# One core, Sinkhorn-sorted block attention into a max-of-two expert layer: the kernel rebuilt with the sort's data stationary, no DRAM scratch and the experts as a linear part plus one ReLU

## The chip, the cores and the metric

The kernel runs on one core of a Trainium2 chip. The metric is the device time of one execution in microseconds. A profile is one execution recorded by the hardware profiler. Names used below: TensorE (PE; its loads of the stationary operand are listed as PEld), VectorE (DVE), ScalarE (ACT), GpSimd (POOL), SyncE (SP). TensorE multiplies a stationary operand, loaded first, with a moving one and writes to PSUM; DVE and ACT take the result from there ("evacuate" it). DMAs are issued from the queues of SP, ACT and POOL; POOL's here also convert float32 to bfloat16.

## The reference

```python
# q, k, v: (4, 8, 768, 64); sort_net: (4, 8, 8, 8); eight blocks of 96 rows
P = sort_net
for _ in range(5):
    P = np.exp(P - np.max(P, axis=-1, keepdims=True))
    P = P / (np.sum(P, axis=-1, keepdims=True) + 1e-09)
    P = P / (np.sum(P, axis=-2, keepdims=True) + 1e-09)
k_sorted = np.einsum('bhij,bhjcd->bhicd', P, k_b)      # v_sorted likewise
scores = scale * q_b @ k_sorted^T                       # inside each block of 96
attn = softmax(scores);  out = attn @ v_sorted
x = out.transpose(0, 2, 1, 3).reshape(3072, 512)
h1 = x @ w1;  h2 = x @ w2                               # (512, 1024) each
return np.maximum(h1, h2) @ w_out                       # (1024, 512), float32
```

## The kernel before

There are 32 groups (batch and head) of 8 blocks. **Sinkhorn** (L69 to L85): all 32 groups on partitions, five rounds of one exp on ACT and six small operations on DVE. **Block-diagonal matrices** (L87 to L98): each group's 8x8 matrix is put on the diagonal of one of two 128x128 tiles (16 groups each) by a DMA of its own, 32 in all, from SP and ACT. **Sort** (`emit_sort_batch`, L142): rows of k and v (16 groups x 8 blocks = 128 partitions, a block's 96 x 64 elements along the row) are the moving operand in pieces of 512 columns, the block-diagonal tile the stationary one. The result, `sort_ps`, has blocks on partitions, which attention cannot use; it is evacuated (k by ACT, L176, v by DVE, L179), written to a DRAM scratch in bf16 (L181) and read back with the 96 rows of a block on partitions (`k_grp` L207, `v_grp` L215).

**Attention** (`emit_attention_group`, L197), a group at a time: four transposes of q (`tq_ps`, L224) and four of k (`tk_ps`, L236), copied by DVE; then twice four scores matmuls (`sc_ps`, L252), one exp on ACT (L260), four matmuls with v and a column of ones (`o_ps`, L264), whose last column is the row's sum, and copy, reciprocal and multiply on DVE (L272 to L274) into `x_stage`. After a batch's eight heads, `emit_x_transpose` (L283) makes `xT`, with the model dimension on partitions.

**Experts**: `emit_moe_h` (L300) takes 512 tokens and 128 of the 1024 hidden columns: four matmuls of 512 columns with w1 (L305), four with w2 (L313), a copy of h1 on ACT (L321), the maximum on DVE (L323). `emit_moe_out` (L326) multiplies with w_out in eight matmuls (L331), copies on ACT (L339) and stores 128 rows. The expert work of finished batches is dealt between the attention of the next ones, one unit at each half group; what is left runs after the last batch. The order on each engine is set by the framework's scheduler from this program order; PSUM has three pools (three sort or h tiles, three transposes or scores, two outputs).

## Time and profile before

| | |
|---|---|
| time, median of three runs | 294.71 us (292.66 to 296.38) |
| span of the profiled execution, first to last instruction | 290.0 us |
| PE busy | 211.6 us, 73%, 1520 matmuls |
| DVE, ACT, POOL busy | 116.6, 99.3, 40.4 us |
| HBM read, written | 31.47 MB, 12.58 MB |

The profiled execution's own time is its span of 290.0 us; the median of the runs is 4.7 us above it. The profile's page cuts the span into 40 slices of 7.25 us and gives the busy share of each engine in tenths, and the clock that TensorE was granted ("PEclk", 9 is full, 5 is half). Rows of a group read: line, engine, operation, what it writes and reads, shapes, count, then busy us, mean ns of one, and the idle time of the engine before them with who ended it. Matmuls are pipelined, so a single one's length contains latency; the pace is read from many in a row.

### The profile page before, as it was taken

What the parts mean: (1) busy time and instruction counts of PE and PEld (TensorE: products, weight loads), DVE (VectorE), ACT (ScalarE), POOL (GpSimd) and SP (SyncE); (2) the same over time, 40 slices, a digit from 0 to 9 for tenths busy, and PEclk for the clock granted to TensorE, in tenths of its full rate; (3) what the DMA queues carried; (4) which work ended last, traced back from release to release, by engine and by line L of the source; (5) the groups of instructions that cost most, each with busy time, mean ns of one, the idle gap of its engine ahead of it and who ended that gap; (6) DMA issues with size and microseconds to landing.
All of it is one profiled execution on the core that took longest, in us unless ns stands there. A gap on an engine that the chain in (4) does not pass through costs nothing.

```text
span 290.0 us, 4264 instructions
## 1 busy us (share of the span) xinstructions
PE 211.6 (73%) x1520; PEld 107.2 (37%) x1520; DVE 116.6 (40%) x393; ACT 99.3 (34%) x198; POOL 40.4 (14%) x66
## 2 busy tenths in 40 slices
PE   0001424235238589998879999999999999999994
PEld 0000000012024365554446455455455554444441
DVE  5400004323027872675352756365645640430320
ACT  2000421003312235434346343357444374333322
POOL 8300402106320121112111212112000000000000
PEclk9999955557555755999997999999999999999999
DMA  9993699999999997546883465754421003003003
GB/s 66 176 213 63 124 218 260 218 180 187 220 219 232 187 139 61 58 57 68 128 141 43 54 70 54 147 109 48 51 75 72 2 0 132 14 0 146 0 27 120
DMA packets 90245, 31.75 MB, mean 109 GB/s; under 512 B 77424, under 2 KB 84592, under 8 KB 90224
## 3 DMA queue, kind: packets, MB, share of 16 engines
q0 software_dynamic: 29120, 12.59, 36.2%
q1 hardware_dynamic: 30576, 9.45, 14.7%
q10 hardware_dynamic: 30528, 9.44, 14.4%
q8 instruction: 12, 0.20, 0.3%
q14 instruction: 9, 0.07, 0.1%
HBM read 31.47 MB, written 12.58 MB: 152 GB/s over the span
## 4 chain that ended last, share of the span: by engine, by line
PE 61%; DMA 24%; DVE 6%; ACT 5%; issue 2%; ACTq 1%; SPq 0%; DVEq 0%
PE h_ps L305 15%; PE moe_o_ps L331 15%; PE h_ps L313 14%; DMA k_sorted_dram<-k_ck 8%; PE o_ps L264 5%; DMA bd<-p_bf 5%; PE sc_ps L252 5%; DMA v_grp<-v_sorted_dram 4%; DMA k_grp<-k_sorted_dram 4%; PE xt_ps L287 3%; DMA v_sorted_dram<-v_ck 2%; PE tk_ps L236 2%; ACT e_sb L260 2%; DVE v_ck L179 1%; ACT k_ck L176 1%
## 5 line engine op out<-in xcount | busy, mean ns | idle before, releaser
L305 PE MATMUL h_ps<-xT,w_sb 128*128 128x512 bf16 x192 | 55.2, 390 | 0.0
L323 DVE TENSOR_TENSOR g_sb<-h_ps,h_sb 128x512 bf16<-128x512 f32 x48 | 33.1, 691 | 53.6 <-PE h_ps L313 51.6
L313 PE MATMUL h_ps<-xT,w_sb 128*128 128x512 bf16 x192 | 53.0, 380 | 0.0
L260 ACT ACTIVATE e_sb<-sc_ps 96x384 bf16<-96x384 f32 x64 | 30.1, 486 | 47.0 <-PE sc_ps L252 34.2
L331 PE MATMUL moe_o_ps<-wout,g_sb 128*128 128x512 bf16 x192 | 44.5, 379 | 0.7 <-ACT o_sb L339 0.7
L321 ACT CAST h_sb<-h_ps 128x512 bf16<-128x512 f32 x48 | 28.2, 588 | 47.8 <-PE h_ps L305 47.6
L164 PE MATMUL sort_ps<-k_ld,bd 128*128 128x512 bf16 x24 | 12.1, 562 | 37.3 <-DMA bd<-p_bf 20.3
L264 PE MATMUL o_ps<-v_grp,e_sb 96*96 96x65 bf16 x256 | 24.7, 224 | 11.6 <-DMA v_grp<-v_sorted_dram 6.4
L203 POOL DMA_DIRECT2D q_grp<-in_q_dram x24 | 18.5, 773 | 104.0 <-PE tq_ps L224 60.4
L179 DVE CAST v_ck<-sort_ps 128x512 bf16<-128x512 f32 x24 | 15.6, 685 | 41.7 <-PE sort_ps L164 34.7
L264 PEld LDWEIGHTS <-e_sb 96*96 96x96 bf16 x256 | 19.9, 138 | 30.1 <-ACT e_sb L260 13.9
L176 ACT CAST k_ck<-sort_ps 128x512 bf16<-128x512 f32 x24 | 13.3, 589 | 44.8 <-DMA bd<-p_bf 19.6
L274 DVE TENSOR_TENSOR x_stage<-o_ps,rs_sb 96x256 bf16<-96x256 f32 x64 | 26.7, 418 | 1.1
L331 PEld LDWEIGHTS <-g_sb 128*128 128x128 bf16 x192 | 18.4, 98 | 21.3 <-issue 1.6
L339 ACT COPY o_sb<-moe_o_ps 128x512 f32<-128x512 f32 x24 | 14.1, 586 | 35.2 <-PE moe_o_ps L331 35.1
L164 PEld LDWEIGHTS <-bd 128*128 128x128 bf16 x48 | 5.4, 121 | 51.8 <-issue 51.6
L313 PEld LDWEIGHTS <-w_sb 128*128 128x128 bf16 x192 | 17.5, 98 | 16.7 <-issue 0.2
L272 DVE COPY rs_sb<-o_ps 96x4 f32<-96x4 f32 x64 | 9.7, 153 | 32.3 <-PE o_ps L264 31.9
L305 PEld LDWEIGHTS <-w_sb 128*128 128x128 bf16 x192 | 17.2, 101 | 13.2 <-issue 0.3
L252 PE MATMUL sc_ps<-qT,kT 64*96 64x96 bf16 x256 | 19.0, 228 | 2.0 <-DVE kT L245 2.0
L252 PEld LDWEIGHTS <-kT 64*96 64x96 bf16 x256 | 12.8, 132 | 17.4 <-DVE kT L245 11.1
L233 DVE COPY qT<-tq_ps 128x384 bf16<-128x384 bf16 x32 | 11.1, 348 | 19.4 <-PE tq_ps L224 19.4
(33 smaller groups left out, 144.5 us busy)
## 6 DMA issues: line engine op xcount, KB each, us to landing
q_grp<-in_q_dram POOLq DMA_DIRECT2D x32, 96.0 KB, 3.3
k_ld<-in_k_dram POOLq DMA_DIRECT2D x6, 512.0 KB, 8.6
v_ld<-in_v_dram POOLq DMA_DIRECT2D x6, 512.0 KB, 11.0
k_sorted_dram<-k_ck SPq DMA_DIRECT2D x24, 128.0 KB
v_sorted_dram<-v_ck ACTq DMA_DIRECT2D x24, 128.0 KB
k_grp<-k_sorted_dram SPq DMA_DIRECT2D x32, 96.0 KB
v_grp<-v_sorted_dram ACTq DMA_DIRECT2D x32, 96.0 KB
out_dram<-o_sb SPq DMA_DIRECT2D x12, 256.0 KB
```

The costliest lines, as they stand in the source:

```text
L164: nc.tensor.matmul(ps, bd_tiles[t], ld[:, sub * SORT_CHUNK : (sub + 1) * SORT_CHUNK], start=True, stop=True,)
L179: nc.vector.tensor_copy(out=ck, in_=ps)
L203: nc.gpsimd.dma_start(out=q_grp, in_=q_g[g].rearrange("(j c) d -> c j d", j=NB))
L252: nc.tensor.matmul(sc_ps[:, sub, :], kT[ii * D : (ii + 1) * D, pr, :], qT[ii * D : (ii + 1) * D, pr, :], start=(sub == 0), stop=(sub == 3),)
L260: nc.scalar.activation(out=e_sb, in_=sc_ps, func=AF.Exp, scale=scale)
L264: nc.tensor.matmul(o_ps[:, sub, :], e_sb[:, sub, :], v_grp[:, i, :], start=(sub == 0), stop=(sub == 3),)
L274: nc.vector.tensor_tensor(out=x_stage[:, par:NB:2, h * D : (h + 1) * D], in0=o_ps[:, :, 0:D], in1=rs_sb.to_broadcast([BLK, 4, D]), op=ALU. ...
L305: nc.tensor.matmul(h1_ps, w_sb[dmt][:, fi * 128 : (fi + 1) * 128], xT[:, dmt, tok0 : tok0 + TCH], start=(dmt == 0), stop=(dmt == 3),)
L313: nc.tensor.matmul(h2_ps, w_sb[dmt][:, DFF + fi * 128 : DFF + (fi + 1) * 128], xT[:, dmt, tok0 : tok0 + TCH], start=(dmt == 0), stop=(dmt ...
L321: nc.scalar.copy(out=h1_sb, in_=h1_ps)
L323: nc.vector.tensor_tensor(out=g_sb, in0=h2_ps, in1=h1_sb, op=ALU.max)
L331: nc.tensor.matmul(o_ps, g_tiles[fi][:, tsi * 128 : (tsi + 1) * 128], wout_sb[fi], start=(fi == 0), stop=(fi == NFT - 1),)
```

## The change

The kernel is rebuilt around the same mathematics. The main parts:

- **Sort.** The block-diagonal matrix becomes the moving operand and the data the stationary one, so that the result comes out transposed. k is loaded with the even heads of eight head pairs on partitions 0 to 63 and the odd ones on 64 to 127. `sort_k` takes one row position at a time, 64 rows x 64 columns stationary against 64x64 moving, alternately for the two halves, into opposite quarters of the output: 384 matmuls; their evacuation puts 16 positions at a time into `kT`. `sort_v` takes one element of the head dimension at a time, 128 x 96 stationary with a step of 64 elements, against 128x128: 128 matmuls into `v_sb`, rows of a block on partitions. The DRAM scratch and the transposes of k are gone.
- **Block-diagonal matrices** come from two small matmuls with a selection matrix and masked multiplies on DVE; the 32 DMAs are gone.
- **q** is loaded in one DMA a batch, six rows to a partition, paired by heads with two DVE copies, and transposed 128 x 128 (24 matmuls a batch).
- **Attention** works on a head pair and four blocks at once: eight scores matmuls (`scores`), one exp over 96x768, eight matmuls with v (`values`), one reciprocal and one multiply; eight transposes for a pair (`x_transposes`), copied by ACT.
- **Experts.** max(h1, h2) = h2 + relu(h1 - h2), so the output is x (w2 w_out) + relu(x (w1 - w2)) w_out. w2 is transposed (32 matmuls), the product formed once (32 matmuls of 512 columns), the difference taken by DVE in place of w1. `moe_h` has four matmuls of 384 columns for each 128 hidden columns and one ReLU for two such; `moe_out` twelve matmuls of 512 columns, four of them with the product.
- **PSUM** is one ring of four tiles of two banks for every use. Who evacuates (`evac`, `pick`) is settled when the program is written out, by running sums of estimated work of ACT and DVE; exps and x copies are always ACT's, the attention's multiplies DVE's.
- **Order** is the program's own, on every engine: batches 0 and 1 of attention with the weight products first, then the expert units of all batches, with the sorts and attention of batches 2 and 3 dealt between the units of batches 0 and 1, and the units of 2 and 3 at the end. The rest of the loads (second half of k and v, q of batches 2 and 3) stand on POOL's queue behind the first ones.

On SP's queue, at the start of the program, before (bd: the block-diagonal tiles; k_sorted_dram: the scratch):

```order
L65 DMA p_sb<-in_sort_net_dram 32x64
L95 DMA bd_107<-p_bf 8x1x8 x8
L95 DMA bd_109<-p_bf 8x1x8 x8
L181 DMA k_sorted_dram<-k_ck 128x512 x12
L207 DMA k_grp<-k_sorted_dram 96x8x64 x8
```

and the whole of SP's queue now:

```order
L580 UNCONDITIONAL_BRANCH
L89 DMA p_sb<-in_sort_net_dram 32x64
L472 DMA out_dram<-o 128x2x512 x11
L468 DMA out_dram<-o_2570 128x512
L468 DMA out_dram<-o_2585 128x512
```

SP is left with the input of Sinkhorn and the stores. What replaces the 32 DMAs stands on DVE, after the last Sinkhorn step (sel: the selection matrix, pe: its product in PSUM, bv and bk: the block-diagonal matrices for v and k):

```order
L176 TENSOR_TENSOR p_bf<-p_sb,colsum 32x64
L185 TENSOR_REDUCE maskJ<-ident 128x8
L193 COPY sel_155<-ident 32x64 x2
L206 TENSOR_TENSOR pm_160<-pe,maskJ 128x64
L213 TENSOR_REDUCE pt_162<-pm_160 128x8
L215 TENSOR_TENSOR bv_164<-mask_101,pt_162 128x128
L222 TENSOR_TENSOR bk_166<-bv_164 128x64
```

The same six kinds follow once more for the second half. On TensorE, the sort before (the last of the first twenty-two sort matmuls, then the transposes of k):

```order
L164 LDWEIGHTS bd_107
L164 MATMUL sort_ps<-v_ld,bd_107 128x512
L236 LDWEIGHTS k_grp
L236 MATMUL tk_ps<-ident,k_grp 128x96
L236 LDWEIGHTS k_grp
```

and now, the end of the key sort, which runs into the scores with no transposes between:

```order
L262 LDWEIGHTS k_raw
L262 MATMUL k_ps<-bk_166,k_raw 64x64
L301 LDWEIGHTS kT
L301 MATMUL s_ps<-qT,kT 96x96
L301 LDWEIGHTS kT
```

The stationary operand is the data now, and a load of it stands ahead of every matmul as before. On TensorE among the experts, the place of an x transpose now (e: the exps, x: the normalized output of attention):

```order
L325 LDWEIGHTS e
L325 MATMUL o_ps<-v_sb,e 96x65
L353 LDWEIGHTS x
L353 MATMUL tx_ps<-ident,x 128x96
L353 LDWEIGHTS x
```

Eight matmuls with v are followed at once by the eight transposes that need their evacuated result; before, the 32 transposes of a batch came in its last group and after it, some of them between matmuls of that group.

The diff, cut to its core (lines of before first, then the new kernel in its own order):

```diff
-    for g in range(G):
-        t, gl = divmod(g, GB)
-        eng = nc.sync if g % 2 == 0 else nc.scalar
-        eng.dma_start(
-            out=bd_tiles[t][8 * gl : 8 * gl + 8, 8 * gl : 8 * gl + 8],
-            in_=p2_bf[g : g + 1, :, :],
-        )
...
-    k_sorted_dram = dram_pool.tile([G * NB, BLKD], BF16, tag="ksd", name="k_sorted_dram")
-    v_sorted_dram = dram_pool.tile([G * NB, BLKD], BF16, tag="vsd", name="v_sorted_dram")
...
-            nc.sync.dma_start(
-                out=k_grp,
-                in_=k_sorted_dram[g * 8 : g * 8 + 8, :].rearrange(
-                    "i (c d) -> c i d", d=D
-                ),
-            )
...
+    psum = ctx.enter_context(tc.tile_pool(name="psum", bufs=4, space=bass.MemoryType.PSUM))
+    ctx.enter_context(tc.manual_schedule())
...
+    load = {"A": 0.0, "D": 0.0}
+    def pick(a_ns, d_ns):
+        if load["A"] + a_ns <= load["D"] + d_ns:
+            load["A"] += a_ns
+            return "A"
+        load["D"] += d_ns
+        return "D"
+    def evac(out_ap, in_ap, n, two_x=False):
+        if pick((200 + n) / 1.2, (130 + (n / 2 if two_x else n)) / 0.96) == "A":
+            nc.scalar.copy(out=out_ap, in_=in_ap)
+        else:
+            nc.vector.tensor_copy(out=out_ap, in_=in_ap)
...
+    k_src = k.rearrange("b (a par) (j c) d -> par (b a) j (c d)", par=2, j=NB)
...
+    load_q(0)
+    load_k(0, 3)
+    ident = const.tile([128, 128], BF16, tag="ident", name="ident")
+    make_identity(nc, ident)
...
+    load_v(0)
+    load_q(1)
+    load_w(w2_sb, moe_w2)
+    load_w(wo_sb, moe_w_out)
+    load_w(w1_sb, moe_w1)
...
+        sel = const.tile([G, 2, 8, NB], BF16, tag=f"sel{sb}", name=f"sel{sb}")
+        src = ident[0:G, sb * 16 : sb * 16 + 16].rearrange("p (gp par) -> p par gp", par=2)
+        for par in range(2):
+            nc.vector.tensor_copy(
+                out=sel[:, par], in_=src[:, par, :].to_broadcast([G, 8, NB])
+            )
+        pe = ps_f32("pe")
+        nc.tensor.matmul(
+            pe[:, 0 : NB * NB],
+            sel.rearrange("p a g j -> p (a g j)"),
+            p_bf.rearrange("p i j -> p (i j)"),
+            start=True,
+            stop=True,
+        )
...
+        nc.vector.tensor_tensor(
+            out=bv,
+            in0=mask16.to_broadcast([128, 16, NB]),
+            in1=pt.to_broadcast([128, NB, 16]).transpose([0, 2, 1]),
+            op=ALU.mult,
+        )
+        bk = const.tile([128, 8, NB], BF16, tag=f"bk{sb}", name=f"bk{sb}")
+        nc.vector.tensor_tensor(out=bk, in0=bv[:, 0:8, :], in1=bv[:, 8:16, :], op=ALU.add)
...
+        for n in range(16):
+            for par in range(2):
+                m = (n + 8 * par) % 16
+                r0 = par * 64
+                nc.tensor.matmul(
+                    ps[r0 : r0 + 64, m * 64 : (m + 1) * 64],
+                    kv[r0 : r0 + 64, t * 16 + m, :],
+                    bd_k[sb][r0 : r0 + 64, :],
+                    start=True,
+                    stop=True,
+                )
+        evac(
+            kT[:, :, t * 16 : (t + 1) * 16],
+            ps.rearrange("p (c m) -> p m c", m=64),
+            1024,
+        )
...
+        for n in range(8):
+            nc.tensor.matmul(
+                ps[0:BLK, n * 128 : (n + 1) * 128],
+                vv[:, :, t * 8 + n],
+                bd_v[sb],
+                start=True,
+                stop=True,
+            )
+        evac(
+            v_sb[:, :, t * 8 : (t + 1) * 8],
+            ps[0:BLK].rearrange("p (d m) -> p m d", m=128),
+            1024,
+        )
...
+        for ii in range(4):
+            i = ih * 4 + ii
+            for h2 in range(2):
+                nc.tensor.matmul(
+                    ps[0:BLK, h2 * 512 + ii * BLK : h2 * 512 + (ii + 1) * BLK],
+                    kT[h2 * 64 : h2 * 64 + 64, gp * 8 + i, :],
+                    qT[b][h2 * 64 : h2 * 64 + 64, hp, :, i * PB : (i + 1) * PB],
+                    start=True,
+                    stop=True,
+                )
...
+        nc.vector.reciprocal(out=rs, in_=ov[:, :, :, 64])
...
+        nc.vector.tensor_tensor(
...
+        nc.scalar.copy(
+            out=xT[:, hp, b * S : (b + 1) * S].rearrange("p (i c r) -> p i r c", r=R, c=PB),
+            in_=ps[:, 0:S].rearrange("p (i r c) -> p i r c", r=R, c=PB),
+        )
...
+            for fb in range(NFB):
+                nc.tensor.matmul(
+                    ps[:, m * 512 : (m + 1) * 512],
+                    w2T[:, fb, dmt * 128 : (dmt + 1) * 128],
+                    wo_sb[:, fb, :],
+                    start=(fb == 0),
+                    stop=(fb == NFB - 1),
...
+    def w_difference(t):
+        nc.vector.tensor_tensor(
+            out=w1_sb[:, 2 * t : 2 * t + 2, :],
+            in0=w1_sb[:, 2 * t : 2 * t + 2, :],
+            in1=w2_sb[:, 2 * t : 2 * t + 2, :],
+            op=ALU.subtract,
+        )
...
+            fb = t * 2 + m
+            for hp in range(HP):
+                nc.tensor.matmul(
+                    ps[:, m * 512 : m * 512 + TCH],
+                    w1_sb[:, hp, fb * 128 : (fb + 1) * 128],
+                    xT[:, hp, tok0 : tok0 + TCH],
+                    start=(hp == 0),
+                    stop=(hp == HP - 1),
+                )
+        g = gpool.tile([128, 2, TCH], BF16, tag="g", name="g")
+        src = ps.rearrange("p (t f) -> p t f", t=2)[:, :, 0:TCH]
+        if pick((200 + 2 * TCH) / 1.2, (130 + 2 * TCH) / 0.96) == "A":
+            nc.scalar.activation(out=g, in_=src, func=AF.Relu)
+        else:
+            nc.vector.tensor_scalar(
+                out=g, in0=src, scalar1=0.0, scalar2=None, op0=ALU.max
+            )
+        g_tiles[b, ch, t] = g
...
+        for hp in range(HP):
+            nc.tensor.matmul(
+                dst,
+                xT[:, hp, tok0 : tok0 + 128],
+                wc[:, hp, :],
+                start=(hp == 0),
+                stop=False,
+            )
+        for fb in range(NFB):
+            nc.tensor.matmul(
+                dst,
+                g_tiles[b, ch, fb // 2][:, fb % 2, off : off + 128],
+                wo_sb[:, fb, :],
+                start=False,
+                stop=(fb == NFB - 1),
+            )
...
+        elif slot == 1:
+            o = opool.tile([128, 2, 512], FP32, tag="o", name="o")
+            evac(o.rearrange("p t n -> p (t n)"), ps, 1024)
+            nc.sync.dma_start(
+                out=out[tok0 - 128 : tok0 + 128, :].rearrange("(t p) n -> p t n", p=128),
+                in_=o,
+            )
...
+        steps = []
+        for u in range(8 + 2):
+            if u < 8:
+                steps.append(lambda u=u: scores(b, u))
+            if u >= 2:
+                steps.append(lambda u=u: values(b, u - 2))
+                if u % 2 == 1:
+                    steps.append(lambda u=u: x_transposes(b, (u - 2) // 2))
+        return steps
+    for half in range(2):
+        q_transposes(0, half)
+    for t in range(6):
+        sort_k(0, t)
+    for u in range(4):
+        scores(0, u)
+    for t in range(8):
+        sort_v(0, t)
+    for u in range(4, 8):
+        values(0, u - 4)
+        scores(0, u)
+        if u % 2 == 1:
+            x_transposes(0, (u - 4) // 2)
+    for half in range(2):
+        q_transposes(1, half)
+    for u in range(4, 8):
+        scores(1, u - 4)
+        values(0, u)
+        if u % 2 == 1:
+            x_transposes(0, u // 2)
+    for t in range(2):
+        w2_transposes(t)
+    for u in range(4, 8):
+        scores(1, u)
+        values(1, u - 4)
+        if u % 2 == 1:
+            x_transposes(1, (u - 4) // 2)
+    for t in range(2):
+        w_product(t)
+    for u in range(4, 8):
+        values(1, u)
+        if u % 2 == 1:
+            x_transposes(1, u // 2)
+    load_q(2)
+    load_k(1, 3)
+    load_v(1)
+    load_q(3)
+    for t in range(2):
+        w_difference(t)
...
+    rest = []
+    for half in range(2):
+        rest.append(lambda half=half: q_transposes(2, half))
+    for t in range(6):
+        rest.append(lambda t=t: sort_k(1, t))
+    for t in range(8):
+        rest.append(lambda t=t: sort_v(1, t))
+    rest += attention_steps(2)
+    for half in range(2):
+        rest.append(lambda half=half: q_transposes(3, half))
+    rest += attention_steps(3)
...
+    units = []
+    for b in range(B):
+        units += [lambda b=b, t=t: moe_h(b, 0, t) for t in range(4)]
+        units += [lambda b=b, t=t: moe_h(b, 1, t) for t in range(4)]
+        units += [lambda b=b, ti=ti: moe_out(b, ti, b == B - 1 and ti >= 4) for ti in range(6)]
+    hold, span = 5, 2 * 14 - 1
+    done = 0
+    for n, unit in enumerate(units):
+        unit()
+        want = len(rest) * max(0, n + 1 - hold) // (span - hold)
+        while done < min(want, len(rest)):
+            rest[done]()
+            done += 1
```

More of the change, by code (lines that the diff above doesn't have):

```diff
@@ L69 @@
+    load_v(0)
[3 more added lines that the diff above has]
+    load_w(w1_sb, moe_w1)
+    rowsum = const.tile([G, NB], FP32, tag="rowsum", name="rowsum")
+    colsum = const.tile([G, NB], FP32, tag="colsum", name="colsum")
+    p_bf = const.tile([G, NB, NB], BF16, tag="p_bf", name="p_bf")
     for it in range(5):
@@ L78 @@
         nc.vector.tensor_tensor(
-            out=p_sb,
+            out=p_bf if it == 4 else p_sb,
             in0=p_sb,
@@ new lines, with scores @@
+    e_tiles, x_tiles = {}, {}
+    def scores(b, u):
+        hp, ih = divmod(u, 2)
+        gp = (b % 2) * 4 + hp
+        ps = ps_f32("s_ps")
+        for ii in range(4):
[5 more added lines that the diff above has]
+                    qT[b][h2 * 64 : h2 * 64 + 64, hp, :, i * PB : (i + 1) * PB],
+                    start=True,
+                    stop=True,
+                )
+        e = epool.tile([BLK, 2, 4 * BLK], BF16, tag="e", name="e")
+        nc.scalar.activation(
+            out=e,
+            in_=ps[0:BLK].rearrange("p (t f) -> p t f", t=2)[:, :, 0 : 4 * BLK],
+            func=AF.Exp,
+            scale=scale,
+        )
+        load["A"] += 800
+        e_tiles[b, u] = e
```

472 lines of the change are left out of this document (192 added, 280 removed).

## The prediction

> **What bounds the kernel now.** I read the page first, then the busy times by stretch, then the chain of waits, then the timeline of TensorE.
>
> ```profile
> span 290.0 us, 4264 instructions
> PE 211.6 (73%) x1520; PEld 107.2 (37%) x1520; DVE 116.6 (40%) x393; ACT 99.3 (34%) x198; POOL 40.4 (14%) x66
> PE   0001424235238589998879999999999999999994
> PEclk9999955557555755999997999999999999999999
> ```
>
> The rows of slices split the span: TensorE (PE) is mostly idle up to about slice 15 and full after it, and in the idle part its granted clock falls to half. Busy times by stretch (columns: stretch, then busy us and instructions of PE, PEld, DVE, ACT, POOL, then granted clock, DMA share, GB/s):
>
> ```profile
> 0.00:113.00 113.00, 43.36 (x275) 21.66 (x276) 36.63 (x135) 25.43 (x53) 26.56 (x48) 0.69 1.07 176
> 99.00:113.00 14.00, 12.07 (x131) 9.77 (x131) 8.68 (x45) 6.04 (x15) 2.31 (x3) 0.50 1.44 116
> 113.00:286.00 173.00, 168.23 (x1248) 85.50 (x1246) 79.94 (x258) 73.28 (x145) 13.88 (x18) 0.98 0.40 66
> ```
>
> For 113 us PE works 43; from 113, where the first expert matmul stands, to 286 it works 168 of 173 at a clock of 0.98. So there are two stages: a first bound by waits, a second bound by PE. The chain of waits names the first one's (start, length, what):
>
> ```profile
> 11.65 5.28 DMA bd<-p_bf
> 22.11 4.54 DMA bd<-p_bf
> ...
> 31.54 7.18 DMA k_sorted_dram<-k_ck
> ...
> 50.98 12.03 DMA k_grp<-k_sorted_dram
> ...
> 78.23 9.80 DMA v_grp<-v_sorted_dram
> ...
> 279.11 6.92 PE moe_o_ps L331 x32
> ```
>
> The block-diagonal matrices go through 32 tiny DMAs, and the sorted keys and values go to DRAM and back. The last row is the price of a large matmul at full clock: 6.92/32 = 0.216 us for 512 columns, so 0.162 for 384 (x 384/512).
>
> **Prices of small matmuls.** Two rows of the timeline before the experts start, one after (start, length, engine, line, count):
>
> ```profile
> 102.22 0.57 PE L252 MATMUL sc_ps<-qT,kT 64*96 64x96 bf16 x8
> 107.20 0.57 PE L252 MATMUL sc_ps<-qT,kT 64*96 64x96 bf16 x8 [0.15 <-DVE kT L245]
> 188.22 0.39 PE L252 MATMUL sc_ps<-qT,kT 64*96 64x96 bf16 x8
> ```
>
> Between the first two lie two groups of 24 small matmuls (4+4 transposes, 8 scores, 8 values) in 4.98 us: 0.104 us each at half clock, short waits included. At full clock: of the 1248 matmuls from 113 to 286, 576 are large (576 x 0.216 = 124.4 us), so the 672 small ones have 173 - 124.4 = 48.6 us, 0.072 each, waits included. Eight scores matmuls, on the two halves of the array's rows, take 0.57 and 0.39 us; scaled from 96 to 64 columns that is 0.048 and 0.032 each, which I take for the new key-sort matmuls (64 columns, alternating between two quarters of the array). Their upper ends are 0.104 and 0.072.
>
> **Prices of evacuations.** Groups by line (count, then busy us and mean ns of one):
>
> ```profile
> L323 DVE TENSOR_TENSOR g_sb<-h_ps,h_sb 128x512 bf16<-128x512 f32 x48 | 33.1, 691 | 53.6 <-PE h_ps L313 51.6 <-ACT e_sb L260 1.3
> L260 ACT ACTIVATE e_sb<-sc_ps 96x384 bf16<-96x384 f32 x64 | 30.1, 486 | 47.0 <-PE sc_ps L252 34.2 <-DMA v_sorted_dram<-v_ck 9.7 <-DMA v_grp<-v_sorted_dram 2.0
> L321 ACT CAST h_sb<-h_ps 128x512 bf16<-128x512 f32 x48 | 28.2, 588 | 47.8 <-PE h_ps L305 47.6 <-DVE rs_sb L273 0.2
> L274 DVE TENSOR_TENSOR x_stage<-o_ps,rs_sb 96x256 bf16<-96x256 f32 x64 | 26.7, 418 | 1.1
> L264 PEld LDWEIGHTS <-e_sb 96*96 96x96 bf16 x256 | 19.9, 138 | 30.1 <-ACT e_sb L260 13.9 <-issue 12.7 <-DVE x_stage L274 0.7
> L245 DVE COPY kT<-tk_ps 128x384 bf16<-128x384 bf16 x32 | 11.2, 350 | 9.8 <-PE tk_ps L236 9.7
> L273 DVE RECIPROCAL rs_sb<-rs_sb 96x4 f32<-96x4 f32 x64 | 10.8, 169 | 0.9
> L76 DVE TENSOR_REDUCE colsum<-p_sb 32x8 f32<-32x64 f32 x5 | 1.3, 253 | 0.2
> L71 DVE TENSOR_REDUCE rowsum<-p_sb 32x8 f32<-32x64 f32 x5 | 1.0, 207 | 2.8 <-ACT p_sb L70 2.8
> ```
>
> ACT costs 102 ns more for 128 more elements, 0.80 ns each: 768 elements 0.79 us, 1024 1.00. DVE costs 273 ns more for 256, 1.07 ns each: 512 elements 0.69, 768 0.96, 1024 1.24; reading bf16 (350 ns for 384) about 0.52 ns each over 0.15 us.
>
> **The change, stage by stage.**
>
> *Start.* The last Sinkhorn step ends at 11.4:
>
> ```profile
> 11.16 0.21 DVE L78 TENSOR_TENSOR p_sb<-p_sb,colsum 32x64 f32<-32x64 f32 x1
> 0.00:10.00 10.00, 0.50 (x4) 0.29 (x4) 5.71 (x34) 2.56 (x6) 8.60 (x18) 1.00 1.11 87
> 10.00:20.00 10.00, 0.00 (x0) 0.00 (x0) 1.41 (x7) 0.00 (x0) 0.00 (x0) 1.00 1.06 206
> ```
>
> The 32 DMAs go. In their place DVE does 13 small operations (about 0.25 each, as L76: 3.3 us), waits twice for one matmul (0.4 each: 0.8), sets a column of ones (0.1) and pairs q's heads in two copies of 1536 elements (between 0.35 and 1.4 each by L245 taken whole or four times; I take 0.75: 1.5). PE starts at 11.4 + 5.7 = 17. Loads: q of batch 0 (0.79 MB as bf16), then k and v of the first half (1.57 MB each), at the 206 GB/s of the second row: v is there by 19 + 2 = 21 us, needed at about 28. POOL's later loads wait there for the readers of q, k and v of the first half; nothing else stands behind them, and all 12.6 MB land by about 65 at that rate, needed from 88. This cover is gone at the 87 GB/s of the first row (a rival, below).
>
> *First stage: attention of batches 0 and 1, no experts.* PE's work: 400 small matmuls (48 q transposes, 128 scores, 128 values, 64 x transposes, 32 w2 transposes), 192 key-sort and 64 value-sort matmuls, 32 large ones for w2 w_out. At which clock? The stretch 99:113 is before's attention without experts: PE busy 86%, clock 0.50. I take half clock for the 400, full for the sorts and the large product, which stand back to back. 400 x 0.104 = 41.6; 192 x 0.032 = 6.1; 64 x 0.072 = 4.6; 32 x 0.216 = 6.9: sum 59.2. Not covered: the last kT and v_sb evacuations (1.3 each), four exps of 0.79 with four PSUM slots (1.5), the x transposes that follow the values at once (reciprocal 0.17, multiply 0.69, hand-over 0.15: 1.0 each; six of eight have a scores unit of about 0.5 between, so 6 x 0.45 + 2 x 1.0 = 4.7), and the subtraction w1 - w2 on DVE, for which every later h matmul waits (2048 bf16 elements twice, 1.2 each by L245's rate, 2.2 by L323's: 2.6): 11.4. The stage takes 70.6 us and ends at 87.6. ACT and DVE have 16 exps, 16 values, 8 x copies, 14 sort evacuations and some 12 us besides: 12.6 + 13.8 + 6.3 + 15.4 + 12.4 = 60.5, 30 each: hidden.
>
> By the Trainium skill (TensorE: Matmul & The Clock Gate, Part 1) about 3.4 us of sustained work releases the full clock, which here would mean all 400 at 0.072 and a time of 231 (rival 1); Part 4 of that page says transposes do not count as work in that sense. The trace's 86% busy at 0.50 agrees with the second statement more than with the first.
>
> *Second stage: experts, with batches 2 and 3 dealt between.* 256 h matmuls x 0.162 = 41.5; 288 output matmuls x 0.216 = 62.2 (x times the product adds 96 to the 192); 432 small x 0.072 = 31.1; 192 key-sorts x 0.032 = 6.1: 140.9. Seven x transposes stand right behind their values: 7 x 1.0 = 7. Sum 148; ends at 235.6. ACT and DVE: 32 ReLUs x 0.87, twelve outputs 13.3, the attention half 55: 96 us, 48 each: hidden. Large matmuls against before: 124.4 there, 41.5 + 62.2 + 6.9 = 110.6 here.
>
> *End.* One row tile, as before: before's last matmul ends at 286.0 (279.11 + 6.92, the chain's last row above) of 290.0, so 4.0 us. The stores, 13 in place of 24, all go through SP's queue, which holds nothing else by then.
>
> Sum: 17 + 70.6 + 148 + 4 = 239.6 of span. The runs' median is 294.71 against a profiled span of 290.0; with the same 4.7 us the forecast is **244**.
>
> **Bounds.** All of the first stage at half clock (sorts too): 192 x 0.016 + 64 x 0.032 = 5.1 more, 249. Key sorts at 0.072 in both stages: 384 x 0.04 = 15 more, 259. Pair copies at either end, w1 - w2 at 2.2: -1 to +3.
>
> **Rivals.**
> 1. *The first stage runs at full clock.* For it: the order has longer stretches of one kind than before, and the clock rises within 4 us of the first large matmuls:
>
> ```profile
> 113.00:115.00 2.00, 2.00 (x12) 0.91 (x10) 0.71 (x2) 0.57 (x2) 0.77 (x1) 0.50 0.31 49
> 115.00:117.00 2.00, 2.00 (x17) 1.14 (x16) 0.20 (x1) 0.97 (x2) 0.00 (x0) 0.89 1.28 98
> ```
>
> Against: 99:113. Price: 400 x 0.032 = 12.8 less: 231. Chance 0.28.
>
> 2. *Strided operands are slow.* The value sort's stationary operand takes every 64th element of a row, and the sort evacuations read PSUM with steps of 64 and 128 elements. Before has no such load; L76, which reads with a step, costs 46 ns more for 64 elements than L71, 0.7 ns each. If a weight load of 138 ns (L264, PEld) doubles and becomes the matmul's pace, 128 x (0.276 - 0.072) = 26 us, and the evacuations (1.74 us each, 28, two engines) pass the key sorts by 2: 272. Chance 0.14. The Trainium skill (SBUF — State Buffer, section on Door 1) speaks against the change here: an access that leaves a 16-byte line pays a penalty, and PSUM's lines are 8 bytes. It gives no price, and no matmul operand of before has such a step, so the trace can't decide.
>
> 3. *The loads come late.* At 87 GB/s v lands at 47 instead of 28: 18 more, 262. Against: the slow row holds q in pieces of 64 elements; q now comes in 384. Chance 0.07.
>
> 4. *The one PSUM ring serializes PE and the evacuations: slower than before.* Every tile, whatever its use, takes the next of four slots, so a late evacuation holds up all of PE. Waits of PE:
>
> ```profile
> PE sort_ps L164 <- ACT k_ck L176: 20.4, 12, 5.5
> PE moe_o_ps L331 <- ACT o_sb L339: 0.7, 2, 0.3
> ```
>
> The first row shows it in before's sort (three slots, 20.4 us in 12 waits, though with a DMA behind it), the second shows two slots that hardly cost anything. All evacuations are 60.5 + 96 = 156.5 us; with half of them exposed the time is 244 + 78 = 322. It passes 300.6, 2% above before, from 36% exposed. Chance 0.06.
>
> **The numbers.** Forecast 0.45, rivals as named. Rivals 1 and 2 and most of 3 lie within 224 to 270, which with the forecast's own 236 to 259 holds over 8 in 10; beyond lie rival 4 and the worse ends of 2. What a measurement can tell from no change here is about 2%, 288.8 to 300.6: faster 0.92, same 0.03, slower 0.05.
>
> **What would show it.** PE's first dense work at about 17 us; the first h matmul near 88 (76 if rival 1 holds, and then PEclk at 9 throughout; 5 in slices 4 to 14 if not); in the value sort, PEld of about 138 ns or, for rival 2, twice that; from the first h matmul 148 us to the last output matmul at a clock near 1.0, with PE busy over 90%. PE waiting for ACT or DVE evacuations by more than 30 us in all would show the ring. I am wrong if the second stage is not bound by PE.

## The result

The new kernel takes 243.54 us (median, 243.13 to 244.06); the kernel before took 293.69 us in runs beside it. The ratio is 0.831, 95% interval 0.827 to 0.835: 17% faster, against a forecast of 244 us. Single executions of a kernel can be 1 to 2% longer at a lower granted clock; the medians and ratios below are of the others. The profiled execution took 243.13 us, of which its span is 241.1.

The page of the kernel after:

```profile
span 241.1 us, 4147 instructions
PE 194.1 (81%) x1846; PEld 128.2 (53%) x1858; DVE 88.2 (37%) x159; ACT 110.3 (46%) x98; POOL 18.1 (8%) x35
PE   0037697867869579999999677898979999999983
...
PEclk9999655575758959999999979999999999999999
```

PE is busy half of the time or more from slice 3 on (18 us); before, that was so from slice 12 on (87 us). The clock is reduced mainly in slices 4 to 14, where it lies between half and full. The busy times by stretch, cut where the first dense work (17), the first h matmul (86.1) and the end of the last matmul (237.4) stand:

```profile
0.00:17.00 17.00, 1.08 (x9) 0.83 (x10) 10.37 (x46) 2.56 (x6) 10.76 (x24) 1.00 0.93 163
17.00:86.10 69.10, 52.71 (x683) 43.87 (x682) 31.10 (x49) 41.06 (x33) 7.38 (x12) 0.69 0.79 144
86.10:237.40 151.30, 140.28 (x1157) 83.55 (x1168) 46.74 (x65) 66.06 (x60) 0.00 (x0) 0.97 0.11 41
237.40:241.10 3.70, 0.00 (x0) 0.00 (x0) 0.00 (x0) 0.58 (x1) 0.00 (x0) 0.97 0.18 71
```

The stages end where they were expected: PE's first transposes at 16.4 (17 forecast), the first stage at 86.1 (87.6), the last matmul at 237.4 (235.6), 3.7 us to the end (4.0). What fills the stages differs from the sum. The groups that show it (line, engine, operation, count, then busy us and mean ns):

```profile
L361 ACT COPY xT<-tx_ps 128x768 bf16<-128x768 bf16 x16 | 43.5, 2722 | 25.2 <-PE tx_ps L353 25.2
...
L279 PEld LDWEIGHTS <-v_raw 128*96 128x96 bf16 x128 | 21.6, 257 | 0.5
L279 PE MATMUL v_ps<-bv,v_raw 128*96 128x128 bf16 x128 | 21.7, 347 | 0.0
...
L83 ACT CAST kT<-k_ps 128x1024 bf16<-128x1024 f32 x7 | 7.0, 1012 | 3.5 <-PE k_ps L262 3.5
L262 PE MATMUL k_ps<-bk,k_raw 64*64 64x64 bf16 x384 | 6.8, 193 | 0.0
L85 DVE CAST kT<-k_ps 128x1024 bf16<-128x1024 f32 x5 | 5.9, 1221 | 2.4 <-PE k_ps L262 2.4
```

The x copies take 2.72 us where the sum had 0.79; the value sort's loads 257 ns; the sort's evacuations 1.01 and 1.22 us, as reckoned from contiguous rows, in spite of their steps in PSUM. The pace of the sorts is read from the timeline (start, length, count), the clock there from the stretches (third number from the end):

```profile
19.05 3.24 PE L262 MATMUL k_ps<-bk,k_raw 64*64 64x64 bf16 x192
...
27.27 10.76 PE L279 MATMUL v_ps<-bv,v_raw 128*96 128x128 bf16 x64
...
111.92 4.02 PE L279 MATMUL v_ps<-bv,v_raw 128*96 128x128 bf16 x24
```
```profile
30.00:40.00 10.00, 8.69 (x57) 8.50 (x56) 6.20 (x6) 2.04 (x2) 2.20 (x4) 0.50 1.18 207
110.00:120.00 10.00, 10.00 (x57) 7.75 (x56) 2.67 (x3) 2.59 (x3) 0.00 (x0) 1.00 0.14 52
```

A key-sort matmul takes 0.017 us (0.032 forecast). A value-sort matmul takes 0.168 us in the first stage, at a clock of 0.50, and 0.168 in the second, at 1.0: the array's clock does not set its pace. That its load does is what experiment 2 tests. What PE waited for:

```profile
PE tx_ps L353 <- DVE x L338: 12.8, 17, 1.6
...
PE o_ps L325 <- ACT xT L361: 2.5, 2, 1.5
...
PE s_ps L301 <- ACT xT L361: 1.7, 2, 0.9
...
PE tx_ps L353 <- ACT xT L361: 0.8, 1, 0.8
```

### The profile page after: what moved, and what is told of

Same layout as the page of the kernel before. It is cut to its first block, busy times and chain, and to the rows that moved or that the text cites. A ratio compares the mean times of both kernels' runs of the same rounds, so it can differ in the third digit from the quotient of the medians.

```text
span 241.1 us, 4147 instructions
## 1 busy us (share of the span) xinstructions
PE 194.1 (81%) x1846; PEld 128.2 (53%) x1858; DVE 88.2 (37%) x159; ACT 110.3 (46%) x98; POOL 18.1 (8%) x35
## 4 chain that ended last, share of the span: by engine, by line
PE 67%; DVE 15%; ACT 12%; issue 4%; DMA 1%; DVEq 0%; ACTq 0%
PE out_ps L458 17%; PE h_ps L422 16%; PE v_ps L279 9%; PE out_ps L450 8%; ACT xT L361 7%; DVE x L338 5%; PE o_ps L325 3%; PE wc_ps L395 3%; PE s_ps L301 3%; PE tx_ps L353 2%; PE tq_ps L239 2%; PE k_ps L262 2%; ACT kT L83 2%; PE tw_ps L375 1%; DVE o L85 1%
## 5 line engine op out<-in xcount | busy, mean ns | idle before, releaser
L361 ACT COPY xT<-tx_ps 128x768 bf16<-128x768 bf16 x16 | 43.5, 2722 | 25.2 <-PE tx_ps L353 25.2
L422 PE MATMUL h_ps<-xT,w_sb 128*128 128x384 bf16 x256 | 47.1, 341 | 1.0 <-DVE w_sb L405 0.9
L458 PE MATMUL out_ps<-wo_sb,g 128*128 128x512 bf16 x192 | 45.4, 379 | 0.1
L309 ACT ACTIVATE e<-s_ps 96x768 bf16<-96x768 f32 x32 | 26.0, 845 | 12.2 <-PE s_ps L301 12.2
L458 PEld LDWEIGHTS <-g 128*128 128x128 bf16 x192 | 18.8, 98 | 22.7
L432 ACT ACTIVATE g<-h_ps 128x768 bf16<-128x768 f32 x21 | 17.4, 830 | 24.9 <-PE h_ps L422 24.9
L450 PE MATMUL out_ps<-wc,xT 128*128 128x512 bf16 x85 | 23.3, 379 | 1.4 <-DVE o L85 0.8
L353 PE MATMUL tx_ps<-ident,x 96*128 96x96 bf16 x128 | 12.2, 232 | 13.7 <-DVE x L338 12.8
L338 DVE TENSOR_TENSOR x<-o_ps,rs 96x512 bf16<-96x512 f32 x32 | 22.0, 687 | 1.1
L325 PE MATMUL o_ps<-v_sb,e 96*96 96x65 bf16 x256 | 18.9, 225 | 4.1 <-ACT xT L361 2.5
L279 PEld LDWEIGHTS <-v_raw 128*96 128x96 bf16 x128 | 21.6, 257 | 0.5
L279 PE MATMUL v_ps<-bv,v_raw 128*96 128x128 bf16 x128 | 21.7, 347 | 0.0
L85 DVE CAST v_sb<-v_ps 96x1024 bf16<-96x1024 f32 x10 | 12.2, 1221 | 21.9 <-PE v_ps L279 21.6
L434 DVE TENSOR_SCALAR g<-h_ps 128x768 bf16<-128x768 f32 x11 | 10.5, 958 | 21.0 <-PE h_ps L422 21.0
## 6 DMA issues: line engine op xcount, KB each, us to landing
k_raw<-in_k_dram POOLq DMA_DIRECT2D x12, 256.0 KB, 12.2
```

The costliest lines, as they stand in the source:

```text
L85: nc.vector.tensor_copy(out=out_ap, in_=in_ap)
L279: nc.tensor.matmul(ps[0:BLK, n * 128 : (n + 1) * 128], vv[:, :, t * 8 + n], bd_v[sb], start=True, stop=True,)
L309: nc.scalar.activation(out=e, in_=ps[0:BLK].rearrange("p (t f) -> p t f", t=2)[:, :, 0 : 4 * BLK], func=AF.Exp, scale=scale,)
L325: nc.tensor.matmul(ps[0:BLK, h2 * 512 + ii * 65 : h2 * 512 + (ii + 1) * 65], e[:, h2, ii * BLK : (ii + 1) * BLK], v_sb[:, h2 * 64 + gp * 8 ...
L338: nc.vector.tensor_tensor(out=x.rearrange("p i t d -> p t i d"), in0=ov[:, :, :, 0:D], in1=rs.to_broadcast([BLK, 2, 4, D]), op=ALU.mult,)
L353: nc.tensor.matmul(ps[:, i * BLK : (i + 1) * BLK], x[:, ii].rearrange("p t d -> p (t d)"), ident[0:BLK, 0:BLK], is_transpose=True, start=True,
```

## The experiments

Theory A is the prediction's picture with the two prices put right: PE sets the pace, so a change is worth what it takes off PE and off PE's waits. Theory B is that ACT, DVE and the PSUM ring set it. Each ratio below is to the kernel before, run on the same chip beside it; differences in us are to the new kernel's 243.54. The kernel before had medians of 292.42 to 293.69 us beside these runs, so about 1 us of such a difference means nothing.

**1. x copies in runs.**

```diff
-            out=xT[:, hp, b * S : (b + 1) * S].rearrange("p (i c r) -> p i r c", r=R, c=PB),
+            out=xT[:, hp, b * S : (b + 1) * S].rearrange("p (r i c) -> p i r c", r=R, c=PB),
...
+    out_rows = out.rearrange("(b p r) n -> b p r n", b=B, r=R)
...
-                out=out[tok0 - 128 : tok0 + 128, :].rearrange("(t p) n -> p t n", p=128),
+                out=out_rows[b, :, ti - 1 : ti + 1, :],
```

> The x copies on ACT write every sixth element (a step of 12 bytes) and take 2.72 us where the sum had 0.79. Here xT holds a batch's tokens in the order (row within six, block, sixteenth), so that the copy writes runs of 16 elements, and the stores put the rows back in place (two rows, 4 KB, together). Theory A (TensorE sets the pace, the copies matter only where PE waits for them, 5.0 us in the profile): the copy falls to about 0.8 to 1.0 us, ACT's busy time by some 28 us, the time by 3 to 7 us, to 237 to 240. Theory B (the slow copies clog the one PSUM ring and lie behind most of PE's 30 us of waits): 15 us or more, to 228 or below. If the write step is not what makes the copy slow, it stays near 2.7 us and the time near 243.

Measured: 237.59 us, ratio 0.810 (0.806 to 0.815), 6.0 us less than the new kernel. The group in this run:

```profile
L361 ACT COPY xT<-tx_ps 128x768 bf16<-128x768 bf16 x16 | 12.8, 799 | 31.2 <-PE tx_ps L353 31.2
```

The write step of 12 bytes was the whole excess: 2722 ns become 799. The copies cost ACT 30.7 us less, the time falls by 6.0: theory A. The waits for xT are gone, those of the x transposes for DVE are not (13.9 us here).

**2. The value sort's operand without the step.** It reads other elements than it should, so the values sorted are not the right ones.

```diff
-                vv[:, :, t * 8 + n],
+                v_raw[:, (t * 8 + n) * BLK : (t * 8 + n + 1) * BLK],
```

> The value sort takes 96 neighbouring elements of a row as its stationary operand, not every 64th element; the values sorted are then the wrong ones, all else is as it was. Theory A (the step makes the load slow, 257 ns, and the load sets the pace of 0.17 us a matmul): the load falls to about 140 ns, as for the 96-column operand of the attention's second product, the pace to about 0.07 to 0.1, and the time by 8 to 12 us, to 231 to 236. Theory B (this matmul form costs 0.17 us whatever the step): load and time unchanged, 243.

Measured: 233.06 us, ratio 0.794 (0.788 to 0.800), 10.5 us less. Group and pace:

```profile
L278 PEld LDWEIGHTS <-v_raw 128*96 128x96 bf16 x128 | 8.7, 134 | 1.5 <-issue 0.7
L278 PE MATMUL v_ps<-bv,v_raw 128*96 128x128 bf16 x128 | 9.2, 233 | 0.5 <-ACT v_sb L83 0.3 <-DVE v_sb L85 0.2
```
```profile
27.14 3.32 PE L278 MATMUL v_ps<-bv,v_raw 128*96 128x128 bf16 x40
```

A load takes 134 ns in place of 257, a matmul 0.083 us in this row in place of 0.168. The clock changes within the row (0.71 on the mean): at 0.50 the matmuls follow each other at 0.107 us, at 1.0 at 0.056, so without the step the array's clock does set the pace. Over both stages the value sort takes 9.2 us of PE in place of 21.7, 12.5 less, of which the time shows 10.5. Theory A; the step, not the form of the matmul, is slow.

**3. Which step.** Two of the eight tiles of the value sort have each step, on a line of their own (steps of 2, 4, 8, 16 elements on L279, L287, L295, L303); the values sorted are again not the right ones.

```diff
-                vv[:, :, t * 8 + n],
...
+                    v_raw[:, n * 96 : n * 96 + 191 : 2],
...
+                    v_raw[:, n * 96 : n * 96 + 381 : 4],
...
+                    v_raw[:, n * 96 : n * 96 + 761 : 8],
...
+                    v_raw[:, n * 96 : n * 96 + 1521 : 16],
```

> The value sort's stationary operand takes every 2nd, 4th, 8th or 16th element (two tiles of eight matmuls each, in both stages; 4, 8, 16, 32 bytes); the values sorted are the wrong ones. If any step doubles the load, all four take about 257 ns. If the cost comes with leaving a line of 16 bytes at each element, the steps of 2 and 4 stay near 134 to 200 and those of 8 and 16 take 257.

Measured: 238.72 us, a single run. The groups of the loads:

```profile
L303 PEld LDWEIGHTS <-v_raw 128*96 128x96 bf16 x32 | 6.0, 275 | 0.1
L295 PEld LDWEIGHTS <-v_raw 128*96 128x96 bf16 x32 | 5.9, 271 | 0.1
L287 PEld LDWEIGHTS <-v_raw 128*96 128x96 bf16 x32 | 3.4, 191 | 0.2
L279 PEld LDWEIGHTS <-v_raw 128*96 128x96 bf16 x32 | 2.5, 142 | 0.5 <-issue 0.3
```

142 ns at 4 bytes, 191 at 8, 271 at 16, 275 at 32, 257 at the kernel's own 128: the price grows up to 16 bytes and then no more, as the second expectation had it. The Trainium skill (SBUF — State Buffer, section on Door 1) gives SBUF lines of 16 bytes and a penalty for each access that crosses to a new one. That the price stops growing at 16 bytes agrees with this; that a step of 8 bytes, two elements to a line, already costs 191 ns in place of 142 does not agree with the two hits a line that the section asks for full bandwidth, and here the measurement decides.

**4. The block-diagonal matrices by 32 DMAs again.**

```diff
-        pe = ps_f32("pe")
...
+    for g in range(G):
...
+        eng = nc.sync if g % 2 == 0 else nc.scalar
+        eng.dma_start(
+            out=bvs[sb][m * NB : (m + 1) * NB, m, :], in_=p_t[g : g + 1, :, :]
+        )
```

The selection matmuls and the masked multiplies go with the removed lines.

> The block-diagonal matrices are filled by 32 small DMAs from SP and ACT again, as in the kernel before; the rest is the new kernel. Theory A (they stand on the path): before they took from 11.6 to 29.4 us, so the key sort starts at about 30 in place of 19, and the time rises by 10 to 14 us, to 254 to 258. Theory B (the values land at about 25 us anyway, and the path goes through the loads): 5 us or less, to 246 to 249.

Measured: 267.21 us, ratio 0.912 (0.907 to 0.916), 23.7 us more: theory A's side, but about twice its size, so neither expectation held. SP's queue, DVE, and PE's longest wait:

```profile
11.50 21.55 SPq L197 DMA_DIRECT2D bv<-p_t  x16
```
```profile
37.53 0.19 DVE L203 TENSOR_TENSOR bk<-bv 128x64 bf16<-128x64 bf16 x1 [8.86 <-DMA bv<-p_t]
```
```profile
PE tq_ps L220 <- DVE q_pair L102: 39.2, 1, 39.2
```

Two things were missed. The sixteen issues on a queue took 21.6 us, with the loads running beside them, instead of the 17.4 of before. And DVE stands in order: the sum bk, which waits for the last DMA, stood ahead of the pairing of q, so not even q's transposes could start. They start at 39.2 in place of 16.4, 22.8 us later, nearly the whole loss. Part of this is the order and not the DMAs: the first half's sum, which the first key sort needs, was ready at 28.7. With the pairing of q ahead of these sums the key sort could have started then, 9.6 us later than the new kernel's 19.05. By this estimate some 10 of the 23.7 us are the DMAs' own; no run separates the two.

**5. max(h1, h2) again.**

```diff
-                    w1_sb[:, hp, fb * 128 : (fb + 1) * 128],
...
+            for wi, wt in enumerate((w1_sb, w2_sb)):
...
+            nc.scalar.copy(out=h1, in_=ps[:, 0:TCH])
...
+            nc.vector.tensor_tensor(
+                out=g[:, m, :], in0=ps[:, 512 : 512 + TCH], in1=h1, op=ALU.max
+            )
```

The two products go into the two banks of one PSUM tile.

> The experts are computed as max(x w1, x w2) w_out again, with a copy on ACT and a maximum on DVE for each 128 hidden columns; no product, no difference. PE has 256 more h matmuls at 0.165 (42 us) and 96 fewer output matmuls at 0.216, no product (8 us) and no w2 transposes (3.6 us): 42.2 - 20.7 - 11.6 = 10 us more. Theory A (PE sets the pace): 8 to 12 us more, 251 to 256. Theory B (the form was chosen by what ACT and DVE have to do, and 64 copies of 0.49 and 64 maxima of 0.56 in place of 32 ReLUs of 0.87 make them the pace): 20 us or more, 263 or above.

Measured: 259.68 us, ratio 0.886 (0.881 to 0.890), 16.1 us more, between the two expectations.

```profile
PE 206.3 (80%) x1954; PEld 139.9 (54%) x1954; DVE 103.5 (40%) x204; ACT 124.6 (48%) x143; POOL 18.1 (7%) x35
```
```profile
PE tq_ps L239 <- DVE q_pair L102: 7.2, 3, 2.5
```

PE is busy 12.2 us longer and idle 3.7 us longer (its span of 257.0 less 206.3, against 241.1 less 194.1; 12 matmuls are missing from the new kernel's records, so its busy time is a little too low). About three quarters are PE's own work. The linear part plus ReLU is thus worth more than the 13.8 us of large matmuls, less 3.3 for the transposes of w2, that the prediction gave it, since it also takes work from ACT and DVE (DVE is busy 103.5 us in place of 88.2). The second row points at DVE: the q transposes wait 7.2 us for its pairing of q in place of 2.5, 4.7 more, which would cover the 3.7. That DVE's extra work is the reason is argued, not shown.

**6. x transposes one unit later.**

```diff
-                if u % 2 == 1:
-                    steps.append(lambda u=u: x_transposes(b, (u - 2) // 2))
+            if u >= 4 and u % 2 == 0:
+                steps.append(lambda u=u: x_transposes(b, (u - 4) // 2))
```

The new lines stand ahead of `values(b, u - 2)`; the order written out for batches 0 and 1 is changed in the same way.

> Every group of x transposes is issued one unit later, so that PE has scores, a product or an expert unit to do while DVE normalizes. Theory A (in-order PE waits for DVE at these places, 12.8 us in the profile, and nothing else takes the wait's place): 8 to 12 us less, 231 to 236. Theory B (the waits move to the next tile of the ring, since ACT and DVE are late as a whole at these places): less than 4 us, 239 to 243.

Measured: 235.20 us, ratio 0.803 (0.798 to 0.809), 8.3 us less, theory A.

```profile
PE tx_ps L353 <- DVE x L338: 5.0, 6, 1.6
```

7.8 of the 12.8 us of this wait are gone, and the time falls by about as much. Little took their place: the q transposes' wait for DVE's pairing grew from 2.5 to 4.7 us.

**7. Both, and a ring of three slots with and without them.**

> The token order that makes the x copies write runs, and the later x transposes, together. If the two save different waits, the gains add: 10 to 18 us less, 226 to 234. If both relieve the same wait (ACT's and DVE's lateness at the x steps), it is no better than the better one of the two by more than 2 us.

Measured: 228.47 us, ratio 0.779 (0.775 to 0.784), 15.1 us less. 6.0 + 8.3 = 14.3: the gains add, so the two saved different waits.

```diff
-    psum = ctx.enter_context(tc.tile_pool(name="psum", bufs=4, space=bass.MemoryType.PSUM))
+    psum = ctx.enter_context(tc.tile_pool(name="psum", bufs=3, space=bass.MemoryType.PSUM))
```

> The PSUM ring has three slots in place of four. If the ring is what couples PE to the evacuations (the prediction's fourth rival), losing a slot shows it: 15 us or more, 258 or above. If PE sets the pace and the slots are ample: less than 6 us, 243 to 249.

> x copies in runs and later x transposes with three PSUM slots in place of four. Losing a slot cost 15 us with the slow x copies. If it was these copies of 2.7 us, holding a slot each, that made the ring tight, it costs 5 us or less now: 229 to 234. If three slots are too few for the order as such, it costs 12 us or more again: 240 or above.

On the new kernel a slot less costs 15.3 us (258.83, ratio 0.880, 0.873 to 0.887); on the one with both changes 5.8 us (234.25, ratio 0.797, 0.790 to 0.804). In the first,

```profile
PE o_ps L325 <- ACT xT L361: 7.6, 5, 2.5
```

has three times its 2.5 us. All of PE's waits for the x copies grew from 5.0 to 12.8 us, about as much as PE's idle time grew (54.7 us in place of 47.0); the rest of that run's loss is PE being busy 4.8 us longer, at a clock of 0.50 instead of 0.62 from 42 to 70 us. The ring does couple PE to the evacuations, as the fourth rival said, and here it was the slow x copies that PE waited for. Without them, and with the transposes later, the same slot is worth little more than a third; how much each of the two changes did for this was not separated.

**8. More matmuls in the first stage.** Six matmuls of 128 columns, read by nobody, after each scores unit of batches 0 and 1.

```diff
+            for h2 in range(2):
+                for n in range(3):
+                    nc.tensor.matmul(ps[:, h2 * 512 + 384 : h2 * 512 + 512], ident, ident, start=True, stop=True)
```

> After each scores unit of batches 0 and 1 stand six more matmuls of 128 columns into unused columns of the same PSUM tile; nothing reads them. They cost PE 96 x 0.055 to 0.107 us = 5 to 10 us. If more matmul work lifts the clock of the first stage from 0.69 to near 1, the gain of up to 12 us pays for them: 236 to 241, and the profile shows the clock. If the clock stays as it is: 246 to 252.

Measured: 249.97 us, ratio 0.854 (0.848 to 0.860), 6.4 us more. The stretch of the attention units, in the new kernel and then in this one:

```profile
42.00:70.00 28.00, 20.75 (x260) 18.32 (x258) 12.66 (x25) 22.57 (x17) 2.01 (x3) 0.62 0.92 168
```
```profile
42.00:70.00 28.00, 22.58 (x328) 20.37 (x329) 13.16 (x25) 19.81 (x16) 2.01 (x3) 0.78 0.92 169
```

In these two traces the clock (third number from the end) rises from 0.62 to 0.78. That the added work raised it is not shown: in the same stretch a slot less in PSUM alone moved it from 0.62 to 0.50 on the new kernel and from 0.69 to 0.79 on the one with experiment 7's changes, and each kernel has one trace. Over the whole span the four runs here were granted 0.896 to 0.923, those of the new kernel 0.887 to 0.894. In any case the added work, 10.2 us of PE, is not paid back: the time is what the second expectation said.

**9. v turned in SBUF.** On top of experiment 7's two changes, eight copies a half write v as element by row, the first half on DVE, the second on POOL; or the second half alone.

```diff
+    def v_turn(sb, t):
+        eng = nc.vector if sb == 0 else nc.gpsimd
+        eng.tensor_copy(
+            out=v_dc[:, t * 8 : (t + 1) * 8, :],
+            in_=v_raw.rearrange("p (c d) -> p d c", d=D)[:, t * 8 : (t + 1) * 8, :],
+        )
...
-                vv[:, :, t * 8 + n],
+                v_dc[:, t * 8 + n, :],
```

> On top of the two changes of the last run (x copies in runs, later x transposes), v is turned in SBUF before the value sort, from row-by-element to element-by-row, in eight pieces of 768 elements: the first half by DVE, between the sort's evacuations, the second by POOL, which has nothing else to do then. The stationary operand is then 96 neighbouring elements. Theory A (a step costs only where TensorE's load reads it or ACT writes it): DVE's pieces take about 0.9 us, the value sort's pace falls from 0.17 to about 0.085 in the second stage (5 us) and is held by DVE's eight pieces in the first (1 to 4 us less): 219 to 223. Theory B (the turning itself pays for the step on DVE or POOL, 2 us or more a piece, and PE waits for it in the first stage): 228 or above.

> The same, but only the second half of v is turned, by POOL; the first half is sorted with the stepped operand as before. Theory A: the second stage gains 5 to 6 us, 222 to 224. Theory B (POOL's copies are too slow to be done before the second value sort, about 50 us after its data are there, or they slow DVE down): 228 or above.

Both halves: 220.57 us, ratio 0.754 (0.748 to 0.760), inside theory A's range. The second half alone: 219.65 us, ratio 0.750 (0.743 to 0.756), a few us below the 222 to 224 of its theory A. The two can't be told apart. Against experiment 7's 228.47 us the turning is worth 8 to 9 us; with its two changes the kernel is 23 to 24 us faster than the new one. Turning v costs DVE and POOL little (both rows from the run with both halves):

```profile
L279 POOL COPY v_dc<-v_raw 128x768 bf16<-128x768 bf16 x8 | 11.5, 1485 | 11.2 <-DMA v_raw<-in_v_dram 11.2
```
```profile
L279 DVE COPY v_dc<-v_raw 128x768 bf16<-128x768 bf16 x8 | 6.7, 897 | 0.3 <-DMA v_raw<-in_v_dram 0.3
```

## Why the prediction was right, and where only its sum was

The mechanism held: the first stage, 113 us of mostly waits, now ends at 86.1, after 16.4 us of start and 70 in which PE is busy for 53, and the second stage is bound by PE (140.3 busy of 151.3 us). Point by point, in us, with what the timeline of the kernel after gives:

| term | forecast | measured | from |
|---|---|---|---|
| start to the first transposes | 17 | 16.4 | timeline |
| key sort, first stage | 6.1 | 3.2 | 192 matmuls |
| value sort, first stage | 4.6 | 10.8 | 64 matmuls |
| product w2 w_out | 6.9 | 8.1 | 31 matmuls recorded, the first few at half clock |
| the 400 small ones | 41.6 | 31.2 | busy 53.3 from 16.4 to 86.1, less the three above |
| not covered, first stage | 11.4 | 16.4 | 69.7 - 53.3 |
| second stage | 148 | 151.3 | stretches |
| of it value sort, key sort | 4.6, 6.1 | 10.9, 3.6 | timeline |
| of it PE idle | 7 | 11.0 | 151.3 - 140.3, with 11 matmuls missing from the records |
| end | 4.0 | 3.7 | stretches |
| around the span | 4.7 | 2.0 | 243.13 - 241.1 |

*Mis-sized terms.* The value sort was taken at 0.072 us and ran at 0.168: 128 x 0.096 = 12.3 us missing. This is the second rival's mechanism, a stationary operand with a step, with half its price. The load did double, 257 ns against the 276 that the rival reckoned with, but the pace is 0.168, less than the length of a load. The other half of that rival, slow evacuations from stepped PSUM, did not happen; nor would the 2 us that it gave them follow from its own figures (12 evacuations x 1.74 / 2 = 10.4 us stay below the key sorts' 384 x 0.032 = 12.3), and its price of 272 lies outside the 224 to 270 into which the prediction counts it. The key sort was 384 x 0.015 = 5.8 us too dear. The x copies were costed at 0.79 and hidden; they took 2.72, of which PE saw some 6 us (experiment 1). The step overlooked was in the code, a write of every sixth element, while the prediction weighed steps of reads only.

*Why these did not move the sum.* The price of 0.104 and 0.072 for a small matmul came from stretches with their waits in it, and the waits were then added once more as "not covered". In the new kernel a stretch at a clock of 0.50 without waits shows the price without them:

```profile
39.34 0.85 PE L325 MATMUL o_ps<-v_sb,e 96*96 96x65 bf16 x8 [1.31 <-DVE v_sb L85]
40.12 0.55 PE L301 MATMUL s_ps<-qT,kT 64*96 64x96 bf16 x8
40.60 0.85 PE L325 MATMUL o_ps<-v_sb,e 96*96 96x65 bf16 x8
```

Sixteen matmuls in 1.26 us (39.34 to 40.60) are 0.079 each, in place of 0.104; the q transposes, with 128 columns, took 0.11. The clock, above half in part of the stage, helped too; the two are not separated. What was too much, 41.6 - 31.2 = 10.4 us in the first stage and some 4 in the second (368 x 0.072 = 26.5 forecast; 140.3 less 10.9, 3.6 and the 103.7 of the large ones leaves 22.1), paid for the value sort and for waits of PE that were longer than counted. The 4.7 us around the span were also too many: the kernel before has about 2 us there as well in its later runs, and the other 2.7 were only that its profiled execution was faster than the median. By the table the terms that were too dear come to 23.9 us and those too cheap to 22.7. That the sum came within about 1 us of the time is luck; the stages and what bounds them are not.

*The clock.* The first stage was taken at half clock except in the sorts and the product. It was granted 0.69 over the stage, 0.50 where the value sort runs, which the prediction had put at full clock; since that sort runs at its load's pace, it made no difference. The first rival (full clock, 231) is refuted as a forecast, and experiment 8 leaves open whether more matmul work raises the clock.

*The third rival* (late loads) did not occur: the loads ran at 209 GB/s from 10 to 50 us, and PE never waited for one.

*The fourth rival* (the ring) did not bring the time above before's, but the ring was tighter than "two slots that hardly cost anything" made it: one slot is worth 15.3 us. PE's waits for ACT and DVE from 16 us on come to some 27 us, just below the 30 that the prediction took as the sign of the ring.

*The parts of the change by experiment.* The on-chip block-diagonal matrices are worth 23.7 us here (with the order that experiment 4 gave the DMAs; some 10 by its estimate without), the expert algebra 16.1. The rest of the way from 293.7 to 243.5 was not undone part by part, since the scratch in DRAM, the sort's new form and the order of attention hang together; their shares stay open. By stage, the spans give 113 - 86.1 = 26.9 us up to the first expert matmul and 173 - 151.3 = 21.7 from there to the last.

## What to carry to other kernels

Price an operand by its step before its size, for every reader and writer. In these runs a step cost nothing (ACT and DVE reading PSUM), doubled the time (TensorE's load) or more than tripled it (ACT writing to SBUF). A price per instruction that comes from a stretch of the trace has that stretch's waits in it; waits may then not be added again. And on an engine that works in order, look at what stands right behind an instruction that must wait: moving each group of eight x transposes one unit later was worth 8.3 us and took no added work.

## What the runs showed of the hardware that was not expected

ACT's copy with a write step of 12 bytes took 2722 ns for 768 elements, with runs of 16 elements 799 ns; ACT's and DVE's reads of PSUM with steps of 256 bytes (`kT`, 1012 and 1221 ns for 1024 elements) and of 512 (`v_sb`, 1021 and 1221) took no longer than the contiguous ones of the output copies in the same trace (1012 and 1225). TensorE's load of 96 columns took 134 ns contiguous, 142 at a step of 4 bytes, 191 at 8, 271 at 16; with the kernel's own step of 128 bytes the value sort kept the same pace of 0.168 us at clocks of 0.50 and 1.0. Matmuls of 64x64 by 64 columns, alternating between two quarters of the array, ran at 0.017 us each, though one of them is listed with 193 ns.

While POOL turned v, DVE's subtraction w1 - w2 slowed down, in the run that turned both halves:

```profile
69.34 4.29 POOL L279 COPY v_dc<-v_raw 128x768 bf16<-128x768 bf16 x3
...
70.75 5.10 DVE L415 TENSOR_TENSOR w_sb<-w_sb 128x2048 bf16<-128x2048 bf16 x2
```

The first of the two subtractions ran beside the last two of POOL's copies and took 3.97 us, ending 1.08 us after the last of them; the second, with POOL done, took 1.21 us, as both do in the kernel after. The h matmuls waited up to 3.5 us for them. This agrees with the Trainium skill (SBUF — State Buffer, section "Who interferes with whom"): a DVE operation with two inputs in SBUF contends with a GpSimd one that reads SBUF, since its second input comes through a read port that they share.
